# Warming products of TensorE made as pairs of 256 columns instead of one of 512

## The chip, the cores and the metric

The kernel runs on one core of a Trainium2 chip. The metric is the device time of one launch in microseconds (us). Most of what follows is read from the profile of one execution: a page of summaries and a trace of every instruction, with five engines: PE (TensorE, matrix products), PEld (its weight loads, which overlap the products), DVE (VectorE), ACT (ScalarE), POOL (GpSimd), and SP, which here only issues transfers. L215 means line 215 of the kernel.

## What is computed

Two layers in a row. The first is causal attention in which each query sees only the six best chunks of 32 keys, ranked by an upper bound from each chunk's minimum and maximum; the second is a soft mixture of eight experts with four slots each.

```python
# attention, per batch (4) and head (8); S = 768, D = 64, chunk = 32, top_k = 6
ub = sum(max(q * k_min, q * k_max), axis=-1)      # per query and chunk, causal chunks only
sel = chunk of j is among the 6 largest ub
scores = where(sel & (i >= j), q @ k.T / sqrt(D), -1e9)
x = softmax(scores) @ v                            # (4*768, 512) over all heads
# soft MoE: 8 experts, 4 slots each, F = 1024
logits = x @ phi
slot_input = softmax(logits, axis=0).T @ x
slot_out[e] = relu(slot_input[e] @ w1[e]) @ w2[e]
out = softmax(logits, axis=1) @ slot_out
```

## The kernel before

The work is cut into 16 pairs of heads (four batches of four pairs). A pair goes through these steps: k and q are transposed on PE (`transposes`, L225) and copied out of PSUM to bf16 (`evac_T`, L235); DVE takes each chunk's minimum and maximum (`kmin` L244, `kmax` L250); `heads` (L256) makes the right-hand side `bd` of the bounds, `qneg` and `qpos` (L264, L272, L274) the left-hand side; `ubound` (L284, L294) makes the bounds on PE; `select` (L305, L307, L308) finds the sixth largest and the mask of chunks left out, `ns_transposes` (L316) and `evac_ns` (L324) turn that mask; `scores` (L334 for q times k, L344 for adding the mask) fills PSUM in six groups, `expo` (L358) takes the exponential on ACT and `mask` (L368) cuts the diagonal blocks on POOL; `pv` (L382) multiplies with v. The weights of the experts come by transfers that POOL issues all along (L150, L160), and the experts' products and the output follow in the last quarter.

Nothing is scheduled by a planner. Each engine executes its instructions in the order in which the program writes them, and the order is written by hand as strings of step names. The string for the first pair is `HEAD`; the function `head` reads one name after the other. `trk:0` and `trq:0` are the transposes of pair 0, `ub:0`, `ns:0`, `sc:0` its bounds, mask transposes and first group of scores, and so on.

Between these steps stand warming products: `w:6` calls `warm(6)`. A warming product multiplies a 128x128 tile of ones (`ones_sq`) with itself, repeated to 512 columns, into a PSUM tile `warm_ps` that nothing reads. It waits for nothing but the ones. The tile is taken from the pool `p_at`, whose one buffer is next taken by `pv`. `HEAD` holds 27 warming products; by the steps around them they stand in eight groups on PE:

| group | products | followed on PE by |
|---|---|---|
| 1 | 7 | `trk:0` (k transposes of pair 0) |
| 2 | 1 | `trq:0` |
| 3 | 6 | `trk:1`, then `ub:0` |
| 4 | 5 | `trq:1`, then `ns:0` |
| 5 | 3 | `sc:2` |
| 6 | 1 | `sc:3` |
| 7 | 1 | `ns:1` |
| 8 | 3 | the first scores of pair 1 |

On PE every product (MATMUL) has a weight load (LDWEIGHTS) of its own ahead of it, also where the weights are the same as before. So 27 warming products are 54 PE instructions.

Of the kernel before, what the change touches and what calls it, by code (L numbers as in the profile page):

```python
# [20 lines left out]
P = 128  # L21
# [38 lines left out]
def kernel(  # L60
# [10 lines left out]
    nc = tc.nc  # L71
# [40 lines left out]
    ones_sq = static.tile([P, P], BF16, name="ones_sq")  # L112
# [97 lines left out]
    warm_ps = p_at.tile([P, 4, P], F32, name="warm_ps", tag="at")  # L210

    def warm(n):
        r = ones_sq.rearrange("p (o c) -> p o c", o=1).broadcast_to([P, 4, P])
        for _ in range(n):
            nc.tensor.matmul(warm_ps, lhsT=ones_sq, rhs=r, start=True, stop=True)  # L215

    def transposes(i, nm, runs=((0, NQT),), home=(p_tp, "tp")):

# [421 lines left out]
    def head(what):  # L640
        name, *arg = what.split(":")
        if setup(name):
            return
        if name in CASTS:
            cast(*CASTS[name])
            return
        i = int(arg[0])
        if name == "w":
            warm(i)
        elif name in ("trk", "trq"):  # L650
            runs = ((0, 3), (3, NQT)) if what == "trk:0" else ((0, NQT),)
            transposes(i, name[2], runs, (p_sc, "sc") if what == "trk:0" or arg[1:] else (p_tp, "tp"))
        elif name in EVAC:
            evac_T(i, EVAC[name], *((nc.scalar.copy, nc.vector.tensor_copy) if what == "evk:0" else ()))
        elif name in DO:
            DO[name](i)
        elif name in ("lk", "lq"):
            load(i, name[1], 2)
        elif name == "sc":
            scores(0, i)  # L660
        elif name == "ex":
            expo(0, i, False)
        elif name == "mk":
            mask(0, i)
# [219 lines left out]
    for n, part in enumerate((high(mneg), mneg_lo)):  # L884
        nc.tensor.matmul(
            lg2, lhsT=part.broadcast_to([NS, P]), rhs=rep.broadcast_to([NS, NQT, NS]),
            start=False, stop=(n == 1), skip_group_check=True,
        )
        nc.tensor.matmul(
            bc, lhsT=part.broadcast_to([NS, P]), rhs=ident[:NS, :NS], start=(n == 0), stop=(n == 1),  # L890
# [181 lines left out]
    n = 0  # L1072
# [41 lines left out]
```

## Time and profile before

| | us |
|---|---|
| median of three runs | 156.06 (155.94 to 156.12) |
| the profiled execution | 155.95 |
| its span, first to last instruction | 154.2 |
| PE busy | 136.8 |
| ACT busy | 121.5 |
| DVE busy | 120.4 |
| POOL busy | 97.5 |

A group of instructions is shown as: line, engine, operation, what it writes and reads, shape, count, busy time and the mean time of one in ns, then the engine's idle time ahead of it and what ended that. In the timeline a row begins with its start and its length in us, both merged over the instructions counted behind the x. The duration of a product includes the way of its columns through the array, so a series of products overlaps with itself: spacing is read from starts. The chain of waits is the work that ended last, followed back step by step.

### The profile page before, as it was taken

The numbers are of one execution on the slowest core, as the hardware profiler recorded it, in microseconds if no ns is written. First come the engines' busy times: TensorE is split into PE (matmuls) and PEld (weight loads), VectorE is DVE, ScalarE is ACT, GpSimd is POOL, SyncE is SP. The second block draws the span as 40 slices with busy tenths as digits, with TensorE's granted clock in tenths as the row PEclk, the third lists the DMA queues.
The fourth block names the chain that finished last, engine by engine and source line by source line (L and its number), as shares of the span: only waits on it lengthen the run. The fifth ranks groups of instructions, "written<-read, shape, count | busy, mean of one in ns | idle before, by whom it ended". The sixth has DMA issues, their size and how long they took to land.

```text
span 154.2 us, 6098 instructions
## 1 busy us (share of the span) xinstructions
PE 136.8 (89%) x2513; PEld 91.6 (59%) x2513; DVE 120.4 (78%) x445; ACT 121.5 (79%) x167; POOL 97.5 (63%) x200
## 2 busy tenths in 40 slices
PE   7889999999999998999999799999989899776700
PEld 2444566767667686666667575767767655453300
DVE  4777988989899998999999999999767551449710
ACT  3678999999999999899999979999997133428700
POOL 6966698974976798885847938794694971000000
PEclk9999999999999999999999999999999999999975
DMA  4999999999999999999999999999999999999996
GB/s 140 207 188 206 206 189 194 215 179 196 209 217 193 199 205 189 198 205 212 205 190 198 209 202 199 206 184 213 217 191 218 211 197 198 181 266 353 371 429 255
DMA packets 45579, 33.31 MB, mean 216 GB/s; under 512 B 26224, under 2 KB 41584, under 8 KB 45296
## 3 DMA queue, kind: packets, MB, share of 16 engines
q0 software_dynamic: 41328, 25.86, 115.4%
q1 hardware_dynamic: 4224, 7.08, 12.5%
q8 instruction: 19, 0.31, 0.7%
q14 instruction: 8, 0.07, 0.1%
HBM read 52.49 MB, written 6.29 MB: 381 GB/s over the span
## 4 chain that ended last, share of the span: by engine, by line
PE 55%; POOL 13%; DMA 9%; DVE 8%; issue 5%; ACT 5%; DVEq 0%; SPq 0%; POOLq 0%; ACTq 0%
PE at_ps L382 12%; PE sc_ps L334 12%; PE sc_ps L344 9%; DMA w_half<-in_moe_w_dram 7%; PE tr_ps L225 6%; PE xT_ps L404 4%; POOL e_sb L368 4%; ACT e_sb L358 3%; PE ub_ps L284 3%; DMA w_sb<-in_q_dram 2%; PE ns_ps L316 2%; POOL v_t L174 2%; DVE o_rows L1029 2%; POOL w_half L160 1%; POOL w_sb L150 1%
## 5 line engine op out<-in xcount | busy, mean ns | idle before, releaser
L358 ACT ACTIVATE e_sb<-sc_ps 128x1024 bf16<-128x1024 f32 (+2 forms) x96 | 83.2, 932 | 4.7 <-PE sc_ps L344 4.5
L368 POOL TENSOR_SCALAR_AFFINE_SELECT e_sb<-e_sb 128x256 bf16<-128x256 bf16 x96 | 37.9, 415 | 15.6 <-ACT e_sb L358 15.2
L334 PE MATMUL sc_ps<-qT,kT 64*128 64x384 bf16 (+3 forms) x260 | 37.5, 306 | 0.7 <-ACT e_sb L358 0.6
L344 PE MATMUL sc_ps<-nsT,smask 64*128 64x384 bf16 (+2 forms) x296 | 37.6, 284 | 0.1
L382 PE MATMUL at_ps<-v_t,e_sb 128*128 128x65 bf16 x630 | 25.9, 193 | 1.0 <-DVE x_sb L395 0.8
L382 PEld LDWEIGHTS <-e_sb 128*128 128x128 bf16 x630 | 22.0, 97 | 5.1 <-issue 4.0
L305 DVE MAX8 mx<-ub_ps 128x8 f32<-128x8 f32 (+1 forms) x192 | 16.9, 165 | 5.6 <-PE ub_ps L294 5.1
L334 PEld LDWEIGHTS <-kT 64*128 64x128 bf16 x260 | 13.5, 93 | 8.4 <-issue 1.8
L174 POOL DMA_DIRECT2D v_t<-in_v_dram x16 | 16.9, 1056 | 1.1 <-PE sc_ps L344 0.9
L344 PEld LDWEIGHTS <-smask 64*128 64x128 bf16 x296 | 14.9, 95 | 3.1 <-issue 0.4
L395 DVE TENSOR_TENSOR x_sb<-at_ps,inv 128x768 bf16<-128x768 f32 (+3 forms) x18 | 15.6, 869 | 0.6
L244 DVE TENSOR_REDUCE mm<-kT 128x24 bf16<-128x768 bf16 x16 | 15.1, 944 | 0.1
L250 DVE TENSOR_REDUCE mm<-kT 128x24 bf16<-128x768 bf16 x16 | 15.1, 943 | 0.0
L235 ACT COPY qT<-tr_ps 128x768 bf16<-128x768 bf16 x16 | 13.0, 813 | 1.5 <-PE tr_ps L225 1.5
L235 ACT COPY kT<-tr_ps 128x768 bf16<-128x768 bf16 (+1 forms) x16 | 12.7, 793 | 0.6 <-PE tr_ps L225 0.6
L150 POOL DMA_DIRECT2D w_sb<-in_moe_w_dram x14 | 10.1, 724 | 0.0
L415 DVE COPY xT_sb<-xT_ps 128x768 bf16<-128x768 bf16 (+1 forms) x16 | 8.6, 535 | 2.0 <-PE xT_ps L404 2.0
L215 PE MATMUL warm_ps<-ones_sq 128*128 128x512 bf16 x27 | 8.7, 446 | 1.1 <-DVE ones_sq L180 1.1
L284 PEld LDWEIGHTS <-qpn 128*128 128x128 bf16 x192 | 6.1, 96 | 4.9 <-issue 3.8
L284 PE MATMUL ub_ps<-bd,qpn 128*128 128x48 bf16 x192 | 7.9, 184 | 0.8 <-issue 0.5
L404 PE MATMUL xT_ps<-ident,x_sb 128*128 128x128 bf16 x96 | 8.4, 220 | 0.0
L1026 ACT ACTIVATE o_rows<-oh_ps,inv_a 128x256 f32<-128x256 f32 x12 | 5.0, 470 | 3.5 <-PE oh_ps L1046 2.7
(171 smaller groups left out, 222.9 us busy)
## 6 DMA issues: line engine op xcount, KB each, us to landing
w_sb<-in_moe_w_dram POOLq DMA_DIRECT2D x14, 1024.0 KB, 18.3
v_t<-in_v_dram POOLq DMA_DIRECT2D x16, 192.0 KB, 15.1
out_dram<-o_rows SPq DMA_DIRECT2D x10, 256.0 KB, 3.0
w_half<-in_moe_w_dram POOLq DMA_DIRECT2D x8, 256.0 KB, 11.2
k_in<-in_k_dram POOLq DMA_DIRECT2D x5, 384.0 KB, 13.3
q_in<-in_q_dram POOLq DMA_DIRECT2D x5, 384.0 KB, 12.3
out_dram<-o_rows SPq DMA_DIRECT2D x1, 1536.0 KB, 6.0
out_dram<-o_rows SPq DMA_DIRECT2D x2, 512.0 KB, 3.9
```

Source lines behind the costliest of these rows:

```text
L174: nc.gpsimd.dma_start(out=v_t[i % NV][:, :, :, :D], in_=v[b, 2 * j:2 * j + 2].rearrange("h (g p) d -> p h g d", p=P),)
L235: copy(t.rearrange("d (p g) -> d p g", g=NQT)[:, :, g0:g1], ps.rearrange("d g p -> d p g"),)
L244: nc.vector.tensor_reduce(mm[:, 0, 0, :], kT, axis=AX.X, op=ALU.min)
L250: nc.vector.tensor_reduce(mm[:, 1, 0, :], kT, axis=AX.X, op=ALU.max)
L284: nc.tensor.matmul(o, lhsT=qpn[:, x, t * P:(t + 1) * P], rhs=bd[:, x], start=(t == 0 and x == 0), stop=False,)
L305: nc.vector.max(mx[:, a, :], ub[:, a, :max(8, 4 * t + 4)])
L334: nc.tensor.matmul(ps[:, h, c:c + w], lhsT=kT[r, kg * P:(kg + 1) * P], rhs=qT[r, qs], start=True, stop=False,)
L344: nc.tensor.matmul(ps[:, h, c + (f - t0) * P:c + (l - t0) * P], lhsT=smask[r, x, kg].rearrange("p a b -> p (a b)"), rhs=nsT[r, (f - x * NJ ...
L358: nc.scalar.activation(e[:, :, :w], st.pop(("scps", i, g))[:, :, :w], func=ACT.Exp, scale=scale)
L368: nc.gpsimd.affine_select(out=e[:, :, c:c + P], in_=e[:, :, c:c + P], compare_op=ALU.is_ge, fill=0.0, base=0, pattern=[[0, 2], [1, P]], ch ...
L382: nc.tensor.matmul(o, lhsT=st["e", i, g][:, h, c:c + P], rhs=v_t[i % NV][:, h, kg, :D + 1], start=(kg == 0), stop=(kg == t),)
L395: nc.vector.tensor_tensor(st["x", b][:, t0:t1, 2 * j:2 * j + 2, :].rearrange("p t h d -> p h t d"), at[:, :, :, :D], inv.broadcast_to([P, ...
```

## The change

Each call `warm(n)` makes 2n products of 256 columns instead of n of 512. They write the two halves of the same PSUM tile in turn. The sum of the columns is the same; the products are 54 instead of 27, and with their weight loads PE has 108 instructions there instead of 54.

```diff
     def warm(n):
-        r = ones_sq.rearrange("p (o c) -> p o c", o=1).broadcast_to([P, 4, P])
-        for _ in range(n):
-            nc.tensor.matmul(warm_ps, lhsT=ones_sq, rhs=r, start=True, stop=True)
+        r = ones_sq.rearrange("p (o c) -> p o c", o=1).broadcast_to([P, 2, P])
+        for x in range(2 * n):
+            nc.tensor.matmul(
+                warm_ps[:, x % 2 * 2:x % 2 * 2 + 2], lhsT=ones_sq, rhs=r, start=True, stop=True)
```

## The prediction

> **What bounds the kernel now.** I read the page first, for which engine is full where.
>
> ```profile
> span 154.2 us, 6098 instructions
> ...
> PE   7889999999999998999999799999989899776700
> ...
> PEclk9999999999999999999999999999999999999975
> ...
> q8 instruction: 19, 0.31, 0.7%
> ...
> L215 PE MATMUL warm_ps<-ones_sq 128*128 128x512 bf16 x27 | 8.7, 446 | 1.1 <-DVE ones_sq L180 1.1
> ```
>
> The profiled execution took 155.95 us: 154.2 us of span and 1.75 us around it. The 27 warming products all lie in the first 18.3 us, so the place to look is the head, not the average. There I read the chain of waits (start, us, what).
>
> ```profile
> 1.31 3.81 DMA w_sb<-in_q_dram
> 5.14 0.82 DVE q_in L581
> 5.97 0.50 DVE kT L235
> 6.57 0.95 DVE mm L244
> 7.53 0.86 DVE mm L250
> 8.87 0.46 PE ub_ps L284 x12
> 9.41 1.07 DVE mx L305 x12
> 10.50 0.47 DVE ns_t L308
> 11.11 0.34 PE ns_ps L316 x3
> 11.47 0.37 DVE nsT L324
> 11.88 0.41 PE sc_ps L344 x4
> 12.31 2.65 ACT e_sb L358 x3
> ...
> 18.14 1.14 POOL e_sb L368 x3
> ...
> 35.58 0.33 PE xT_ps L404 x6
> ```
>
> No row of this chain is L215. Up to 12.3 us the head waits for q to land and then for DVE; the three stretches of PE in it are the bounds, the ns transposes and the first scores. After that ACT and POOL carry it, and PE only from about 33 us, where no warming product is left. The timeline of TensorE shows the warming groups and what follows each (start, us, engine, line, operation; idle time before it and its releaser in brackets).
>
> ```profile
> 1.13 3.17 PE L215 MATMUL warm_ps<-ones_sq 128*128 128x512 bf16 x7 [1.13 <-DVE ones_sq L180]
> 4.51 0.99 PE L225 MATMUL tr_ps<-ident,k_in 128*64 128x128 bf16 x12 [0.21 <-DVE k_in L581]
> 5.44 0.39 PE L215 MATMUL warm_ps<-ones_sq 128*128 128x512 bf16 x1
> 6.02 0.73 PE L225 MATMUL tr_ps<-ident,q_in 128*64 128x128 bf16 x12 [0.20 <-DVE q_in L581]
> 6.69 1.47 PE L215 MATMUL warm_ps<-ones_sq 128*128 128x512 bf16 x6
> 8.09 0.53 PE L225 MATMUL tr_ps<-ident,k_in 128*64 128x128 bf16 x12
> 8.87 0.46 PE L284 MATMUL ub_ps<-bd,qpn 128*128 128x48 bf16 x12 [0.26 <-DVE bd L256]
> ...
> 9.22 1.24 PE L215 MATMUL warm_ps<-ones_sq 128*128 128x512 bf16 x5
> ...
> 11.11 0.33 PE L316 MATMUL ns_ps<-ident,ns_t 128*128 128x128 bf16 x3 [0.19 <-DVE ns_t L308]
> ...
> 15.76 0.27 PE L344 MATMUL sc_ps<-nsT,smask 64*128 64x256 bf16 x2
> 15.87 0.27 PE L334 MATMUL sc_ps<-qT,kT 64*128 64x256 bf16 x2
> 15.98 0.27 PE L344 MATMUL sc_ps<-nsT,smask 64*128 64x256 bf16 x2
> ...
> 17.61 0.81 PE L215 MATMUL warm_ps<-ones_sq 128*128 128x512 bf16 x3
> 18.35 0.39 PE L334 MATMUL sc_ps<-qT,kT 64*128 64x512 bf16 x2
> ```
>
> Of eight groups these are five (the others have 3, 1 and 1 products, at 12.65, 13.83 and 16.96 us). The first four are each followed by work for which PE then waits, 0.21, 0.20, 0.26 and 0.19 us: they are cover for somebody else's delay.
>
> **The change part by part.** It removes 27 products of 512 columns and adds 54 of 256, each with its own weight load, so 27 products and 27 loads more. Columns, operands and the bank written stay. In the instruction streams that both kernels are built to, everything else on PE stands in the same order with the same waits, and the other four engines' streams differ in tile numbers alone. So nothing is moved past anything, no wait is added, and there are three costs: the spacing of the products, the loads, the longer code.
>
> *Spacing.* A product's duration includes the way through the array, so I take starts. The group at 9.22 us has five products in 1.24 us, the last of which takes 0.379 (its median, in the row below): (1.24 - 0.379) / 4 = 0.215 us each. For 256 columns the three rows at 15.76 to 15.98 us start 0.11 us apart, two halves of the array side by side in each. Two steps are 0.22 us, so a pair costs 0.22 - 0.215 = 0.005 us more than one product, which is also about the rounding of these rows. All 27: 0.135 us of PE time.
>
> *Weight loads.* The answer for line 215 gives load and product (ns min/median/max):
>
> ```profile
> L215 PEld LDWEIGHTS <-ones_sq x27: 95/98/152, 1.1 to 17.8; 128*128 128x128 bf16 x27
> L215 PE MATMUL warm_ps<-ones_sq x27: 376/379/634, 1.1 to 18.0; 128*128 128x512 bf16 x27
> ```
>
> A load takes 98 ns against the 107 ns that 256 columns stream at the rate above (0.215 / 2), so it only just fits beneath one product if loads follow each other strictly. They need not: six x transposes, each a full 128x128 weight with 128 columns, take 0.33 us in the chain, 55 ns each, less than one load lasts. So loads overlap at half the new width already, and I take nothing for them. The other end is each added load exposed in full.
>
> The slow start has its own size. The first seven products take (3.17 - 0.634) / 6 = 0.423 us each, twice the later spacing, although the page's granted clock shows 9 there; a half is then 0.21 us against the longest load of 152 ns, which hides too.
>
> *What reaches the end.* Of the 27 extra spacings, 19 lie in the first four groups, 7, 1, 6 and 5. At 0.005 us they cost 0.035, 0.005, 0.03 and 0.025 us against idle times of 0.21, 0.20, 0.26 and 0.19 us, so all is hidden; were the cover gone it would be 19 x 0.005 = 0.1 us. The groups of 3, 1 and 1 run beside ACT's unbroken exponentials (12.31 us on) or ahead of a wait for DVE and POOL. The last three products are the only ones with no cover that I see:
>
> ```profile
> 19.00 2.02 ACT L358 ACTIVATE e_sb<-sc_ps 128x1024 bf16<-128x1024 f32 x2 [0.28 <-PE sc_ps L344]
> ```
>
> Here ACT waits for the scores begun at 18.35 us, right behind them: 3 x 0.005 = 0.015 us, if POOL's chain, which waits for ACT, takes it on.
>
> *Code.* The 19 instruction packets carry 0.31 MB, 16 KB each; 0.31 MB over the 5026 PE rows of the page (2513 + 2513) is 62 bytes a row:
>
> ```profile
> PE 136.8 (89%) x2513; PEld 91.6 (59%) x2513; DVE 120.4 (78%) x445; ACT 121.5 (79%) x167; POOL 97.5 (63%) x200
> ```
>
> 54 instructions are 3.3 KB, a fifth of one packet. So at most one packet more, and the later ones fall some 54 instructions earlier in PE's work. A packet takes 0.7% of 16 engines' span, 0.007 x 16 x 154.2 / 19 = 0.91 us on one DMA engine. That is the largest delay it could give a transfer behind it on that engine. The largest gain is the wait that a transfer causes late in the kernel, POOL's for w_sb ahead of the last half weights:
>
> ```profile
> 127.14 0.74 POOL L160 DMA_DIRECT2D w_half<-in_moe_w_dram  x1 [1.15 <-DMA w_sb<-in_moe_w_dram]
> ...
> 137.63 0.29 PE L1009 MATMUL so_last<-w_half,hT_pad 128*32 128x256 bf16 x4 [0.29 <-DMA w_half<-in_moe_w_dram]
> ```
>
> I take nothing, since the packets keep their number, or nearly, and their size; the ends are -1.15 and +0.91 us.
>
> *Sum.* 155.95 + 0.015 = 155.97 us on the profiled execution. That lies 0.11 us under the median of the three runs, 156.06 (155.94 to 156.12), so on the median it is 156.08, which I give as 156.1 us.
>
> **The rivals.**
>
> *A. The loads are exposed (slower).* Each added product costs a load: seven at 152 ns in the slow start and 12 at 98 ns in the next three groups make 1.06 + 1.18 = 2.24 us on PE before the ns transposes. The idle times listed absorb 0.21 + 0.20 + 0.26 + 0.19 = 0.86; about 1.4 us is left, delays the first exponential at 12.31 us and so POOL's chain: 157.5 us. It decides from 0.86 / 19 = 45 ns for each added product. For it speaks only the 9 ns of margin; against it stand the transposes at 55 ns.
>
> The Trainium skill, "TensorE: Matmul & The Clock Gate", section "Back-to-back issue gap", speaks for such a price: in a real stream of loads and products it gives 81 ns for 128 columns and 131 ns for 512, so two narrow products should cost far more than one wide one. My estimate for 256 columns by these figures is 98 ns, 65 ns more for a pair, 1.8 us of PE time for 27. Neither end agrees with this trace (55 ns and 215 ns), so the measurement decides.
>
> *B. The clock opens later (slower).* The slow spacing ends between the first transposes (12 in 0.99 us) and the next warming product. If pairs counted less as activity and the slow rate lasted through the six products at 6.69 us, these would take 6 x 0.423 = 2.54 instead of 6 x 0.215 = 1.29 us, and the transposes behind them 0.46 us more (0.99 against 0.53); less the 0.26 us of idle time that is 1.45 us: 157.5 us. Against it: pairs leave no more gaps than single products, and the three runs agree within 0.18 us.
>
> The skill's same page, section "Part 1: The HAM clock gate (the "warmup" mystery)", says that the gate looks at time in a window that runs free of the kernel, not at a count of matmuls. By that the pairs change nothing; this trace, one execution, cannot show what the gate counts.
>
> *C. Shifted code packets meet other transfers.* Slower: up to 0.91 us, half of it as a middle, 156.5 us. Faster: a w_sb or half weight lands earlier, up to 1.15 us, of which half is 155.5 us. For it: DMA is busy to the end. Against: a packet is 1/19 of 0.7%, and most loads are issued long ahead of their use.
>
> *D. The change does not do what it says,* one product being split or merged anyway. The streams show 54 products of 256 columns; I give it nothing.
>
> **How the numbers follow.** About 0.2% (0.31 us) is what a measurement of this kernel can tell from no change. The forecast, and whatever of C stays within that, gets 0.74; A 0.09, B 0.03, C beyond the bound 0.06 slower and 0.08 faster. So faster 0.08, same 0.74, slower 0.18. The range goes from 155.7 (half of C's lower end is left out below) to 156.8 us, which takes in most of C and of the unhidden 0.135 us and leaves out A and B (0.12) above: 8 in 10 or a little more.
>
> **What would show it right or wrong.** Right: 54 rows of L215 with 256 columns, groups as long as before within 0.04 us, an idle time still standing before the bounds (8.87 us) and the ns transposes (11.11 us), the exponentials starting at 12.3 us, 19 or 20 instruction packets. A would show warming groups longer by about 0.1 us a product and those idle times gone; B a second group still at 0.21 us a half; C equal times up to some wait on a DMA, and a difference from there. The prediction is wrong if the first exponential moves by more than 0.1 us, or if a wait late in the kernel changes by 0.3 us.

## The result, and the profile after

| | us |
|---|---|
| before, median of 22 runs | 156.31 (155.90 to 158.12) |
| changed, median of 22 runs | 157.41 (156.34 to 159.00) |
| ratio | 1.0055, interval 1.0029 to 1.0080 |
| changed, the profiled execution | 158.92, span 157.2 |

The kernel became slower by 0.55%, 0.86 us on 156.31, with an interval of 0.45 to 1.25 us. The ratio, here and below, is taken from the single runs without those over 1.5% above the fastest of their kernel (two of the 22 after); the quotient of the two medians is 1.0070. The profiled execution, 158.92 us, is one of the slowest of its 22. Two of the losses that its rows show could not be tied to the change. From the page and from the timeline of TensorE in the head:

```profile
span 157.2 us, 6152 instructions
...
PEclk9999999999999999999999999999999959999955
...
q8 instruction: 20, 0.33, 0.8%
...
1.13 3.17 PE L215 MATMUL warm_ps<-ones_sq 128*128 128x256 bf16 x14 [1.13 <-DVE ones_sq L180]
...
7.04 2.74 PE L215 MATMUL warm_ps<-ones_sq 128*128 128x256 bf16 x12
...
10.19 0.47 PE L285 MATMUL ub_ps<-bd,qpn 128*128 128x48 bf16 x12
10.55 1.25 PE L215 MATMUL warm_ps<-ones_sq 128*128 128x256 bf16 x10
```

The third group takes 2.74 us instead of 1.47: its products still run at the slow spacing, (2.74 - 0.421) / 11 = 0.21 us a half, and the fourth at 0.11. The clock record of the trace begins at 9.8 us (5.4 us before), and the bounds start at 10.19 us instead of 8.87. The 5 in the clock row is a second loss: between 125.8 and 129.2 us PE ran at half clock.

```profile
125.80:129.20 3.40, 3.40 (x44) 1.67 (x48) 1.70 (x8) 1.19 (x3) 2.70 (x4) 0.50 1.44 198
```

The late opening did not come back in two further profiles of the changed kernel (e7 and e14 below, at 5.1 and 4.1 us). A stretch of half clock ahead of the kernel's end stands in 13 of the 17 profiles on record, with pairs and without. Runs of the kernel before scatter up to 158.12 us too. What does belong to the change is the third thing on that page, 20 instruction packets instead of 19. The page gives the count; the trace has the times. The last two packets, start and length in us:

```
before   128.1 0.89    134.9 0.95
changed  135.7 0.89    142.7 1.46
```

At 142.7 us SP issues the outputs. The first row is the summary of its issues before (min/median/max in ns), the second after; the third is the one issue that lies in that window after.

```profile
L1050 SPq DMA_DIRECT2D out_dram<-o_rows x11: 505/570/1420, 134.1 to 142.8; - x11
```

```profile
L1051 SPq DMA_DIRECT2D out_dram<-o_rows x11: 439/562/1660, 136.7 to 146.0; - x11
...
142.88 1.66 SPq L1051 DMA_DIRECT2D out_dram<-o_rows  x1
```

An issue takes 0.56 us, this one 1.66. Before, too, one took 1.42 us, the second, at 134.81 us, while the 19th packet came; but there the outputs had only begun. What the later stall does is in the windows of one microsecond (the last column is GB/s, the one before it the DMA engines' share), before and after:

```profile
143.00:144.00 1.00, 1.00 (x10) 0.69 (x11) 0.32 (x2) 0.34 (x1) 0.00 (x0) 1.00 1.02 342
144.00:145.00 1.00, 1.00 (x6) 0.42 (x5) 1.00 (x2) 1.00 (x3) 0.00 (x0) 1.00 1.00 354
```

```profile
143.00:144.00 1.00, 0.91 (x9) 0.44 (x7) 0.83 (x3) 1.00 (x3) 0.00 (x0) 1.00 0.97 327
144.00:145.00 1.00, 0.10 (x2) 0.00 (x0) 1.00 (x2) 0.28 (x1) 0.00 (x0) 1.00 0.35 109
145.00:146.00 1.00, 0.92 (x9) 0.65 (x10) 0.21 (x2) 0.20 (x1) 0.00 (x0) 1.00 0.82 279
```

Before, the outputs leave at 342 GB/s and more in every microsecond from 137 to 152 us, while DVE's last work on them ends at 147.3; the transfers, not PE, end the kernel. After the change there is a hole of most of a microsecond in that stream, and what it lacks comes later.

The same kernel profiled again (157.59 us, run e7 below) has its clock open at 5.1 us, and its chain of waits in the head stands beside that of before:

```profile
8.85 0.46 PE ub_ps L285 x12
...
11.08 0.34 PE ns_ps L317 x3
...
12.29 2.65 ACT e_sb L359 x3
```

Before: 8.87, 11.11 and 12.31 us. With the clock open in time, the head costs nothing.

### The profile page after: what moved, and what is told of

Read it like the earlier page. It is cut to its first block, busy times and chain, and to the rows that moved or that the text cites. A ratio compares the mean times of both kernels' runs of the same rounds, so it can differ in the third digit from the quotient of the medians.

```text
span 157.2 us, 6152 instructions
## 1 busy us (share of the span) xinstructions
PE 139.4 (89%) x2540; PEld 95.2 (61%) x2540; DVE 120.5 (77%) x445; ACT 121.7 (77%) x167; POOL 97.2 (62%) x200
## 4 chain that ended last, share of the span: by engine, by line
PE 65%; POOL 9%; DVE 7%; ACT 7%; issue 5%; DMA 2%; DVEq 0%; ACTq 0%; POOLq 0%
PE sc_ps L335 12%; PE at_ps L383 12%; PE sc_ps L345 8%; PE tr_ps L226 7%; PE xT_ps L405 4%; POOL e_sb L369 4%; ACT e_sb L359 4%; PE h_ps L933 3%; PE ub_ps L285 3%; DMA w_sb<-in_k_dram 2%; PE warm_ps L215 2%; PE ns_ps L317 2%; ACT o_rows L1027 2%; POOL v_t L174 2%; DVE o_rows L1030 2%
## 5 line engine op out<-in xcount | busy, mean ns | idle before, releaser
L215 PE MATMUL warm_ps<-ones_sq 128*128 128x256 bf16 x54 | 10.2, 347 | 1.1 <-DVE ones_sq L180 1.1
L215 PEld LDWEIGHTS <-ones_sq 128*128 128x128 bf16 x54 | 5.8, 120 | 3.8 <-DVE ones_sq L180 1.1
```

The source lines that it names most:

```text
L215: nc.tensor.matmul(warm_ps[:, x % 2 * 2:x % 2 * 2 + 2], lhsT=ones_sq, rhs=r, start=True, stop=True)
```

## The experiments

Three theories stood against each other. 1, code: the 20th packet costs, in the narrow form only where it meets the outputs, in the wide form wherever it comes. 2, clock: pairs make the clock open later. 3, pairs: spacing or loads cost by themselves. In each kernel "p" is a pair step (the change's loop), "t:n" is n products of a single column with loads of their own, "w" is the step of before. Only the word list `HEAD` is edited. The program before has 5021 PE instructions (the page counts 5026 rows, 2513 and 2513), the changed one 5075. A ratio compares with runs of the kernel before on the same chip; experiments on different chips are compared through it.

**e1, pairs in groups 1 to 3.**

```diff
-HEAD = w:6 w:1 ... trk:0 w:1 ... w:4 kmax:0 w:1 ... schunk w:1 trk:1:s ...
+HEAD = p:6 p:1 ... trk:0 p:1 ... p:4 kmax:0 p:1 ... schunk p:1 trk:1:s ...
```

> Pairs in groups 1 to 3 alone (14 of the 27 products), 512 columns in the others: PE has 5049 instructions against 5021 before and 5075 in the changed kernel. Theory 1 (code): the changed kernel's 20th instruction packet, which arrives at 142.7 us in the midst of SP's output issues and makes one of them 1.66 us long instead of 0.57, costs about 0.9 us, and nothing else does. Then this kernel has 19 packets and is within 0.2% of before (ratio 1.000), or, if 28 more instructions are enough for the 20th, it is at 1.005 to 1.006 and shows it. Theory 2 (clock gate): pairs in the groups ahead of the bounds make the clock open a step later more often, 1.3 us each time; then the ratio is 1.004 to 1.008 with 19 packets. Theory 3 (spacing or loads in the pairs): 1.0003.

Measured: 1.0049 (1.0022 to 1.0077). The profile is a clean one, with the clock open from 6.6 us on and no half clock until the end. Three rows of before, on DVE's last scaling of the outputs and on the stream, and then those of e1:

```profile
145.20 2.06 DVE L1029 TENSOR_SCALAR o_rows<-o_ps,inv_b 128x512 f32<-128x512 f32 x3
...
145.00:146.00 1.00, 0.93 (x4) 0.23 (x2) 1.00 (x3) 1.00 (x3) 0.00 (x0) 1.00 1.04 409
...
153.00:154.00 1.00, 0.00 (x0) 0.00 (x0) 0.00 (x0) 0.00 (x0) 0.00 (x0) 0.50 0.00 0
```

```profile
145.49 2.06 DVE L1037 TENSOR_SCALAR o_rows<-o_ps,inv_b 128x512 f32<-128x512 f32 x3
...
143.81 1.52 SPq L1089 DMA_DIRECT2D out_dram<-o_rows  x1
...
145.00:146.00 1.00, 1.00 (x5) 0.34 (x3) 1.00 (x2) 1.00 (x3) 0.00 (x0) 1.00 0.70 253
...
153.00:154.00 1.00, 0.00 (x0) 0.00 (x0) 0.00 (x0) 0.00 (x0) 0.00 (x0) 0.50 0.12 49
154.00:155.00 1.00, 0.00 (x0) 0.00 (x0) 0.00 (x0) 0.00 (x0) 0.00 (x0) 0.50 0.03 12
```

DVE's last work starts 0.3 us later than before, the span is 155.78 us against 154.24, 1.54 more, so about 1.25 us are lost behind the last computation. The packet came at 143.8 us. There is the long issue, the hole in the stream (253 GB/s where before has 409), and at the end a trickle at 0.12 and 0.03 of the 16 engines' share, where all had stopped by 153 us before. By the trace the last three transfers of the stream start alone, at 153.61, 154.07 and 154.53 us, as they would if one DMA engine were behind the others. 28 instructions are enough for the 20th packet.

**e2, pairs in groups 4 to 8.**

```diff
-HEAD = ... ub:0 w:1 spreada w:2 ... w:1 sel:0 w:1 ... (and the eight products behind)
+HEAD = ... ub:0 p:1 spreada p:2 ... p:1 sel:0 p:1 ... (and the eight products behind)
```

> Pairs in groups 4 to 8 alone (13 products), 512 columns in groups 1 to 3: 5047 PE instructions. Theory 1 (code): as for the first run, ratio 1.000 with 19 packets, 1.005 to 1.006 with 20. Theory 2 (clock gate): the clock is open before the pairs begin, so 1.000 in any case. Theory 3 (spacing, group 8 uncovered): 1.0003.

Measured: 1.0013 (0.9981 to 1.0045). With 5047 instructions, two fewer than e1, no issue is long in this profile:

```profile
q8 instruction: 19, 0.31, 0.7%
...
L1058 SPq DMA_DIRECT2D out_dram<-o_rows x11: 468/567/607, 134.8 to 143.7; - x11
```

The trace has a 20th packet at 156.9 us, behind the span of 155.1, and this execution took 157.52 us: 2.42 us lie outside the span, where before has 1.75. Over its 12 runs that part varies from 1.67 to 2.79 us. So at this length the packet sometimes comes behind the outputs, and the end of the program then comes later instead.

**e3, code without pairs.**

```diff
-HEAD = ... spreada w:2 ... evns:1 w:1 ...
+HEAD = ... spreada t:18 ... evns:1 t:9 ...
```

> No pairs at all. Three of the 512-column products behind the bounds (two in group 4, one in group 8) are replaced by nine products of one column each, which take about as long at 25 ns each (225 ns against 215): 48 PE instructions more, 5069. Theory 1 (code): 20 packets and a ratio of 1.005 to 1.006, although nothing is paired. Theory 2 (clock gate) and theory 3 (spacing): 1.000, since the groups ahead of the bounds are those of before.

Measured: 1.0076 (1.0045 to 1.0106), packet at 142.2 us.

```profile
142.59 1.44 SPq L1056 DMA_DIRECT2D out_dram<-o_rows  x1
```

No product is paired, and the loss is there, a little above the forecast of 1.005 to 1.006; theories 2 and 3 had forecast 1.000. This profile has half clock from 141.0 to 147.8 us, but so has that of e8 below (140.6 to 147.5 us), which took 156.49 us.

**e4, longer code.**

```diff
-HEAD = ... w:1 spreada w:2 ... w:1 sel:0 w:1 ... w:2 w:1 ... w:1 evns:1 w:1 evq:2 lw w:1 ...
+HEAD = ... t:9 spreada t:18 ... t:9 sel:0 t:9 ... t:18 t:9 ... t:9 evns:1 t:9 evq:2 lw t:9 ...
```

> No pairs. Eleven of the 512-column products (groups 4, 5 and 8) are replaced by nine products of one column each: 176 PE instructions more, 5197, so that the 20th packet is fetched about 150 instructions before the end, near 135 us, where the 19th lay before, instead of 29 before the end. Theory 1 (code) in its narrow form (it is the place in the output phase that costs): 20 packets, and a ratio near 1.000 (0.998 to 1.003). Theory 1 in its wide form (any additional packet costs its DMA time): 1.005 to 1.006. Theories 2 and 3: 1.000, as long as the one-column products keep the clock open.

Measured: 1.0026 (0.9992 to 1.0059), packet at 137.7 us, no long issue; the profiled execution took 156.16 us. It fits the narrow form, but the interval still holds the change's value: by itself inconclusive.

**e5, e1 with two instructions fewer.**

```diff
-HEAD = p:6 p:1 ... trq:2 w:1 mk:4 ...
+HEAD = p:6 p:1 ... trq:2 mk:4 ...
```

> The kernel of the first run (pairs in groups 1 to 3) with the one product of group 7 left out: two PE instructions fewer, 5047, as many as in the second run. Theory 1 (code, place in the output phase): the 20th packet moves from 143.8 us to behind the last output, no output issue of SP takes over 0.7 us in the last 10 us, and the ratio falls from 1.0049 to 1.000 to 1.002. Theory 2 (clock gate) and theory 3 (pairs as such): the pairs ahead of the bounds are all there, so 1.004 to 1.006 as before.

Measured: 1.0102 (1.0052 to 1.0152) in six runs: a miss. In the profile (157.76 us) the packet came at 157.2 us, 2.56 us lie outside the span, and PE was at half clock from 124.7 to 128.1 us. It was repeated as e12.

**e6, e2 with two instructions more.**

```diff
-HEAD = ... trq:2 p:1 mk:4 ...
+HEAD = ... trq:2 p:1 t:1 mk:4 ...
```

> The kernel of the second run (pairs in groups 4 to 8) with one product of a single column added in group 7: two PE instructions more, 5049, as many as in the first run. Theory 1 (code): the 20th packet moves from behind the outputs to about 143.8 us, one output issue of SP takes about 1.5 us, and the ratio rises from 1.0013 to 1.004 to 1.006. Theories 2 and 3: 25 ns of work, so it stays at 1.001.

Measured: 1.0078 (1.0041 to 1.0114), packet at 145.4 us.

```profile
145.42 1.51 SPq L1095 DMA_DIRECT2D out_dram<-o_rows  x1
```

With one product of a single column more than e2, 1.0078 stands against 1.0013 (the intervals overlap only from 1.0041 to 1.0045; the two were measured on different chips). This profile (159.09 us) also has half clock from 135.7 to 139.1 us.

**e7, the changed kernel again.**

> The changed kernel once more, on the chip of the neighbouring runs, so that its profile can be read at another phase of the clock. Theory 1: 1.005 to 1.008, the 20th packet near 142.5 us with an SP issue of about 1.5 us, whether the clock opens before 7 us or at 9.8 us. Theory 2: the clock opens at 9 us or later in this profile too, and the first exponential starts over 1 us later than before's 12.31 us.

Measured: 1.0055 (1.0021 to 1.0089), packet at 141.5 us, clock open at 5.1 us. The head is quoted above; the issue is the long one:

```profile
141.81 1.38 SPq L1051 DMA_DIRECT2D out_dram<-o_rows  x1
```

The loss is the same with an early clock, so theory 2 is not needed for it.

**e8, the change with longer code.**

```diff
-HEAD = (groups 5 to 8) w:2 w:1 ... w:1 ... w:1 ... w:1 evns:1 w:1 evq:2 lw w:1
+HEAD = (groups 1 to 4 as pairs; 5 to 8) t:18 t:9 ... t:9 ... t:9 ... t:9 evns:1 t:9 evq:2 lw t:9
```

> All pairs of the change in groups 1 to 4; in groups 5 to 8 each product is replaced by nine of one column instead of a pair: 5187 PE instructions, 112 more than the changed kernel. Theory 1 (code, place): the 20th packet falls near 138 us, where the fourth run had it, ahead of the second half of the outputs; the ratio is 1.000 to 1.003, less than the change's 1.0055, although there are more products and the same pairs in the head. Theory 1 in its wide form (every further packet costs) and theories 2 and 3: at least the change's 1.005.

Measured: 0.9988 (0.9948 to 1.0028). 112 instructions more than the change, the same pairs in groups 1 to 4, the packet at 137.5 us, and the loss is gone. Groups 5 to 8 have no pairs here; e2, which has them there, is at 1.0013.

**e9 and e10, code alone, eight instructions apart.**

```diff
-HEAD = ... trq:2 w:1 mk:4 ...
+HEAD = ... trq:2 w:1 t:10 mk:4 ...     (e9; e10 has t:14)
```

> The kernel before with ten products of a single column added in group 7, where PE waits for POOL afterwards: 20 PE instructions more, 5041, nothing paired, nothing left out. Theory 1 (code): still 19 packets, no output issue of SP above 1 us after 138 us, ratio 1.000 (0.998 to 1.002). Theory 2 (clock gate) and theory 3 (pairs as such): also 1.000.

> The same with fourteen such products: 28 PE instructions more, 5049, eight more than in its neighbour, 0.1 us of PE work. Theory 1 (code): 20 packets, one of them near 143.8 us with an SP issue of about 1.5 us, ratio 1.004 to 1.008. Theories 2 and 3: 1.000 as its neighbour.

Measured: e9 1.0037 (1.0007 to 1.0068), e10 1.0109 (1.0068 to 1.0149, six runs), more than the forecast 1.004 to 1.008. The step is there, but e9 was expected at 1.000 with 19 packets, and in its profile (157.59 us) the 20th came at 145.2 us. SP made one short issue meanwhile, 0.34 us as the same one before, and it was not stretched. The end shows another form of the loss, which looks like a single engine that is behind:

```profile
152.00:153.00 1.00, 0.00 (x0) 0.00 (x0) 0.00 (x0) 0.00 (x0) 0.00 (x0) 0.50 0.93 393
...
153.50:154.90 1.40, 0.00 (x0) 0.00 (x0) 0.00 (x0) 0.00 (x0) 0.00 (x0) 0.50 0.04 18
```

A share of 0.04 is less than one engine of 16, and it goes on to 154.6 us, 1.4 us after the others stopped at 153.2.

**e11, ten pairs in groups 1 to 3.**

```diff
-HEAD = w:6 w:1 ... trk:0 w:1 ... w:4 kmax:0 w:1 ... schunk w:1 trk:1:s ...
+HEAD = p:6 p:1 ... trk:0 p:1 ... w:4 kmax:0 p:1 ... schunk p:1 trk:1:s ...
```

> Pairs for ten products of groups 1 to 3 (all seven of group 1, the one of group 2, two of group 3): 5041 PE instructions. Theory 1 (code): 19 packets and 1.000 (0.998 to 1.002), with the pairs in the slow start of the clock. Theory 2 (clock gate, pairs count less in the first windows): 1.003 to 1.006. Theory 3: 1.0002.

Measured: 1.0006 (0.9975 to 1.0038), although the profiled execution (158.32 us) has the packet at 150.3 us; its clock opens at 4.6 us. Eight of the 12 runs lie at 155.87 to 157.74 us and make the ratio; four lie at 158.32 to 158.72, and with them the medians differ by 0.23%. Either way pairs are no worse at 5041 instructions than e9 without pairs.

**e12, e5 again.**

> The fifth run once more (pairs in groups 1 to 3, the product of group 7 left out, 5047 PE instructions), which was at 1.0102 in six runs where theory 1 expected 1.000 to 1.002. If that came from leaving out the product of group 7, it is at 1.008 or more again. If it came from the clock's closing in these six runs (its profile has PE at half clock from 124.7 to 128.1 us) and from where the 20th packet lands at this count, it is lower this time, between 1.001 and 1.006.

Measured: 1.0030 (1.0002 to 1.0058) in 12 runs. The profiled execution (156.75 us) has

```profile
q8 instruction: 19, 0.31, 0.7%
```

and no 20th packet anywhere, in the very program that had one at 157.2 us in e5. So near the threshold it depends on the execution whether the packet is fetched and when. The time outside the span says the same of the runs without a profile: it is above 1.9 us in 18 of the 54 runs of the kernels with 5041 and 5047 instructions, and at most 1.86 us in every run of the longer ones. The product of group 7 is not the cause of e5; why all six of its runs lie above 157.7 us stays open.

**e13 to e15, the place.** e14 is the changed kernel, e15 is e8's; e13 lies between.

```diff
-HEAD = (e8, groups 5 to 8) t:18 t:9 ... t:9 ... t:9 ... t:9 evns:1 t:9 evq:2 lw t:9
+HEAD = (e13)               t:10 t:5 ... t:5 ... t:5 ... t:5 evns:1 t:5 evq:2 lw t:5
```

> Pairs in groups 1 to 4, and in groups 5 to 8 five products of one column in place of each product: 5123 PE instructions, 48 more than the changed kernel, 64 fewer than the eighth run. The 20th packet should fall near 140 us, between the changed kernel's 142 and the eighth run's 137.5. If the place costs through SP's issue of the second half of the outputs (139.5 us on), it costs when it meets such an issue: 1.003 to 1.006 with an issue over 1 us in the profile, 0.999 to 1.002 without one. If every 20th packet costs, 1.005.

> The changed kernel, for the difference to its neighbour: 1.004 to 1.008, 20th packet at 141 to 143 us and an SP issue of 1.3 to 1.7 us.

> The eighth run's kernel (5187 PE instructions, packet near 137.5 us) again: 0.998 to 1.003 and no SP issue over 1 us after 138 us, at least 0.3% below its neighbour, if the place costs; 1.004 or more if any 20th packet does.

Measured on one chip: e13 1.0021 (0.9991 to 1.0051), packet at 139.3 us, no issue above 0.66 us; e14 1.0066 (1.0033 to 1.0099), packet at 141.6; e15 1.0003 (0.9971 to 1.0035), packet at 138.1. The same microseconds in e14 and e15:

```profile
142.01 1.60 SPq L1051 DMA_DIRECT2D out_dram<-o_rows  x1
...
143.00:144.00 1.00, 0.24 (x5) 0.06 (x2) 1.00 (x2) 0.42 (x1) 0.00 (x0) 1.00 0.53 178
```

```profile
L1064 SPq DMA_DIRECT2D out_dram<-o_rows x11: 482/565/606, 134.7 to 142.9; - x11
...
143.00:144.00 1.00, 0.87 (x9) 0.65 (x10) 0.27 (x2) 0.15 (x1) 0.00 (x0) 1.00 1.04 348
```

All kernels in order of PE instructions; the packet's time is that of the one profiled execution:

| PE instructions | kernel | pairs | 20th packet, us | ratio |
|---|---|---|---|---|
| 5021 | before | 0 | none | 1 |
| 5041 | e11 | 10 | 150.3 | 1.0006 |
| 5041 | e9 | 0 | 145.2 | 1.0037 |
| 5047 | e2 | 13 | 156.9 | 1.0013 |
| 5047 | e5, e12 | 14 | 157.2, none | 1.0102, 1.0030 |
| 5049 | e1 | 14 | 143.8 | 1.0049 |
| 5049 | e6 | 13 | 145.4 | 1.0078 |
| 5049 | e10 | 0 | 145.7 | 1.0109 |
| 5069 | e3 | 0 | 142.2 | 1.0076 |
| 5075 | changed, e7, e14 | 27 | 142.7, 141.5, 141.6 | 1.0055, 1.0055, 1.0066 |
| 5123 | e13 | 19 | 139.3 | 1.0021 |
| 5187 | e8, e15 | 19 | 137.5, 138.1 | 0.9988, 1.0003 |
| 5197 | e4 | 0 | 137.7 | 1.0026 |

The time rises with the packet's moving into the outputs and falls again when it has passed to their front; the pairs column explains nothing. No kernel beats the one before: e8 and e15 include 1 in their intervals.

The 19th packet moves along with the 20th: to 130 us, ahead of the outputs, in e4, e8 and e15, where it stands at 134.9 us before and at 133.8 to 135.7 in the changed kernel. So the place of the 20th alone was not separated from the number of packets that fall into the outputs; e13, with packets at 134.3 and 139.3 us, has two there and loses at most 0.5%.

Half clock late in the kernel is not what the change costs: the mean granted clock of all runs was 0.9755 in e7 and 0.9747 in e14, and 0.9757 and 0.9726 in their longer counterparts e8 and e15, where the loss is gone.

## Why the prediction was wrong

*Spacing: right, a little too high.* In e7 the fourth group has ten halves in 1.25 us:

```profile
9.20 1.25 PE L215 MATMUL warm_ps<-ones_sq 128*128 128x256 bf16 x10
...
L215 PEld LDWEIGHTS <-ones_sq x54: 95/98/151, 1.1 to 18.0; 128*128 128x128 bf16 x54
L215 PE MATMUL warm_ps<-ones_sq x54: 269/273/421, 1.1 to 18.1; 128*128 128x256 bf16 x54
```

(1.25 - 0.273) / 9 = 0.109 us a half, 0.217 a pair against 0.215: 0.002 us instead of the forecast 0.005.

*Weight loads: right.* At 98 ns beneath 109 ns they stay hidden, in the slow start as well: 14 halves take the 3.17 us that seven products took. Rival A would have shown groups longer by 0.1 us a product; in e7 none is, and on record only the third, at the slow spacing.

*What reaches the end: right for the head.* The idle times ahead of the bounds and the mask transposes stand in e7 at 0.29 and 0.17 us (0.26 and 0.19 before).

```profile
8.85 0.46 PE L285 MATMUL ub_ps<-bd,qpn 128*128 128x48 bf16 x12 [0.29 <-DVE bd L257]
...
11.08 0.33 PE L317 MATMUL ns_ps<-ident,ns_t 128*128 128x128 bf16 x3 [0.17 <-DVE ns_t L309]
```

*Rival B, the clock.* It did open late in the profile on record, and its price was well put: the bounds came 1.32 us later, against the estimate of 1.45. But ten profiles with pairs in the first three groups show it opening at 4.1 to 6.6 us nine times and at 9.8 us once, seven profiles without such pairs at 4.1 to 6.8 us, and e11, with ten pairs in these groups, is at 1.0006. That the pairs make it likelier is not shown.

*Code: this is the step that failed.* The prediction allowed one packet more, priced it at up to 0.91 us, and then took nothing for it and gave a loss beyond the bound a chance of 0.06. The measured 0.86 us (0.0055 x 156.31) is nearly the whole of that price. This term of the sum, put at nothing, is the one that cost. That the two figures are so close is partly luck. The price was the delay of a transfer behind the packet on one DMA engine, and only the lone last transfers of e1, e6, e9, e10 and e11 look like that; in the changed kernel the profiles show an SP issue 0.8 to 1.1 us longer than the usual 0.56 and no such engine at the end. Nor was the price the upper bound that it was meant to be: e3 lost 1.2 and e10 1.7 us (1.06 by the lower end of its interval). Three things were missed. The step "at most one packet more" was not followed up: 5021 instructions lie just under a boundary, since 20 more can be enough (e9, e11), and the question when the 20th would be fetched has an answer, at the end of PE's program, where the outputs are written. The trace of before already had a sign of it, an SP issue of 1.42 us while the 19th packet came. And "half of it as a middle" had no ground: at the end of the kernel the transfers are the bound, so what delays them there delays the end. The range ended at 156.8 us, inside this rival's own price (156.06 + 0.91 = 156.97), and so excluded what happened, 157.41 us. Of what still lies between the two, 0.25 us is the start of the sum: the median before was 156.06 us in three runs and 156.31 in 22.

The Trainium skill, "Runtime: NRT & Kernel Launch", section "Instruction fetch mechanics", says that instructions come in blocks of 16 KiB by the sequencer's own DMA queue and that crossing a boundary is "mostly hidden". The packets agree in size. What the first 19 cost, no run here shows; the 20th, with 0.86 us, is an exception that the "mostly" leaves room for.

Two things stay open. Why SP's issue lasts about a microsecond longer beside a packet was not tried apart, and so the step from the packet to the loss is read from profiles and not tested. The issue was longer beside the 20th packet in seven profiles (on record, e1, e3, e6, e7, e10, e14), and not in e9 and e13, where an issue overlapped with it too; beside the 19th, too, some were longer (1.42 us before, 1.15 in e9) and others kept to 0.55 to 0.62 us (e2, e10, e13). And the half-clock stretches late in the kernel go with the scatter of single runs: of the 29 runs of before beside e7, the 16 with a mean granted clock of 0.978 or more have a median of 156.2 us, the other 13 one of 157.1. Their cause was not looked for.

## What to carry to other kernels

A program's length is a quantity with steps in it: one more block of instructions is one more transfer, and what it costs depends on what runs when it is fetched, not on what was added. Before calling additional instructions free, count them against the last packet in the trace, and look whether the next one would fall into a stretch that transfers bound. Where it does, a longer program can be faster than a shorter one: 112 instructions more took the loss away (1.0066 against 1.0003 on one chip, 1.0055 against 0.9988 on another).

## What the runs showed that was not expected

Two instructions out of 5049 can move the time by 0.65% (e2 to e6, 1.0013 to 1.0078); the test in the other direction, two fewer than e1, did not show it (1.0049 to 1.0102 and, in more runs, 1.0030). Near the threshold the 20th packet is no property of the program: the same program fetched it at 157.2 us in one execution and not at all in another (e5, e12). The loss shows in three forms: a stretched issue of SP (1.38 to 1.66 us instead of 0.56), last transfers that start alone, as of one DMA engine that ends 1.4 us (e9) or 1.8 us (e11) behind the others, and, behind the last output, time outside the span (2.42 us instead of 1.75 in e2).
